# Attention and a token/channel mixer on one core: three stretches of small tiles in two steps, value products in seven pieces

## The chip, the cores and the metric

The kernel runs on one core of one Trainium2 chip. The metric is the device time of one execution in microseconds (us). Engines are named as in the profile: PE (TensorE, matrix products), DVE (VectorE), ACT (ScalarE), POOL (GpSimd) and SP (SyncE, which here only issues DMAs).

## The reference

A squared-ReLU attention over 8 batches, 12 heads, 448 positions and head size 64 feeds a mixer that works first over positions (tokens), then over channels.

```python
def _attn_ref(q, k, v):                      # (8, 12, 448, 64)
    scores = scale * np.matmul(q, k.transpose(0, 1, 3, 2))
    attn = np.maximum(scores, 0.0) ** 2 / S
    return np.matmul(attn, v).astype(np.float32)

def _moe_ref(x, w_tok1, w_tok2, w_ch1, w_ch2):   # x: (8, 448, 768), heads side by side
    xt = x.transpose(0, 2, 1)
    h = np.maximum(xt @ w_tok1, 0.0) @ w_tok2    # 448 -> 256 -> 448
    u = x + h.transpose(0, 2, 1)
    h2 = np.maximum(u @ w_ch1, 0.0) @ w_ch2      # 768 -> 1536 -> 768
    return (u + h2).astype(np.float32)
```

## The kernel before

**Steps.** The attention is cut into 24 steps of four heads; three steps make a batch. The operations of a step have short names that the text uses:

- `ld` loads q, k and v (POOL's queue, with the cast to bf16, two halves of 64 partitions each).
- `T` transposes q and k on PE for steps 0 to 7; its copies `cp` bring them from PSUM into `kqT`. From step 8 (`QDMA`) an interleaving copy on DVE (`i`) and a DMA transpose on SP (`x`) do this.
- `S` is a score tile, seven in a step (`KC`): four 64x64 products that run at once on the four quarters of PE and fill two PSUM banks. Each bank is emptied by a ReLU on ACT or DVE (`r`, lines 338 and 340), and DVE squares the pair (`q`, line 608) in one of 13 `sq` buffers.
- `V` is the value product: 28 products of 64x64 over the seven chunks, summed in two banks (line 629). In the kernel before it is one unit that needs all seven squares. Two evictions `xe` write `xT`.
- The token part: a transpose of `xT` (`X` on PE, from step 9 (`XDMA`) the DMA transpose `xd`), `t1` (line 745), `t2` (line 775), and the sum `u` on DVE; `ub` transposes u back by DMA on SP for the end.

**Channel part.** For each batch 12 products `C1` (line 837; six 128x128 matmuls of 448 columns each), and for each pair of batches 14 products `C2` (line 910; twelve matmuls a half). DVE adds u (line 926) and the result is stored (line 894). This is the large pool of work with 128x128 tiles that fills PE between the stretches of small tiles.

**The order.** The order of each engine's instructions is written by a planner (`Planner.run`, time steps of 0.01 us) when the kernel is built. Each operation has a duration, dependencies, and for DMAs a model of the rings that POOL and SP feed. PE's choice knows two shapes, "s" (64x64 tiles: T, S, V) and "m" (128x128). In shape "s" it goes on with values and scores that are ready and find banks; in shape "m" it takes large units until `since`, the time with large work, passes a bound that falls with the channel work in stock (between `FGAP` 0.5 and `GAP` 6 us), and then enters a stretch. The chip executes each engine's queue in the order so fixed, with semaphores where one engine needs another.

**Start and end.** In step 0 the first half of q comes by SP in fp32 (`load_first`, cast on DVE and ACT), the rest by POOL; the transposes of q and k of a half share a bank. The last output tile is stored in three pieces, each in two halves of partitions.

Of the kernel before, what the change touches and what calls it, by code (L numbers as in the profile page):

```python
# [18 lines left out]
QLATE, XLATE = 4.0, 6.0  # L19
FRONT, LOOKP, LOOKV = 40.0, 0.0, 0.0  # L20
VCUT = {}
RANKS = {}
CP_DVE = ()
# [3 lines left out]
HOLD = 1  # L27
STOCK, SLOPE, FGAP = 10.0, 0.4, 0.5
# [6 lines left out]
class Op:  # L35
    def __init__(self, name, eng, emit, deps=(), **kw):
        self.name, self.eng, self.emit = name, eng, emit
        self.deps = [d for d in deps if d is not None]
        self.on = None
        self.start = self.seen = None  # L40
        self.banks = 0
        self.bank = []
        self.frees = None
        self.rank = 0
        self.shape = None
        self.work = None
        self.durs = None
        self.late = None
        self.drain = self.adds = 0.0
        self.slack = 0.3  # L50
        self.__dict__.update(kw)
# [5 lines left out]
class Planner:  # L57
# [28 lines left out]
    def run(self, stream, gap, enter, tol, lanes=8):  # L86
# [27 lines left out]
        idle, filling = 0.0, None  # L114
        while left:
            self.moved(t, step)
            for e in ("POOL", "SP"):
# [12 lines left out]
                if o.work is not None:  # L130
                    issued[e] += 1
                    self.rings[e].append([t + o.dur + (1.13 if e == "POOL" else 0.135), o.work, o])
# [6 lines left out]
            for e in ("ACT", "DVE"):  # L139
# [3 lines left out]
                for o in self.open["FLEX"]:  # L143
# [4 lines left out]
                    key = (o.rank + (0 if e == o.eng else 100), o.at, o.n)  # L148
# [21 lines left out]
            if free["PE"] <= t:  # L170
# [19 lines left out]
                if shape == "s":  # L190
# [8 lines left out]
                else:  # L199
                    work, k = 0.0, -1  # L200
                    if va is not None and fits(va):
                        work += va.dur
# [37 lines left out]
                else:  # L240
# [5 lines left out]
                    if o is sc:  # L246
                        queue.pop(0)
                    if o is va:
                        values.pop(0)
# [19 lines left out]
def kernel(  # L269
# [84 lines left out]
    def load(s, t, halves=(0, 1)):  # L354
        src = {"k": k, "q": q, "v": v}[t]
        b, i = divmod(s, GS)
        for half in halves:
# [8 lines left out]
            o = add(Op(f"ld{t}{s}.{half}", "POOL", emit, dur=0.585, work=0.645, late=0.2 if s < 2 else None))  # L366
# [25 lines left out]
    def load_wc1(i, parts):  # L392
# [8 lines left out]
        o = add(Op(f"wc1.{i}", "POOL", emit, dur=0.9, work=12.0 / parts))  # L401
# [3 lines left out]
    def load_wc2(i, parts):  # L405
# [8 lines left out]
        o = add(Op(f"wc2.{i}", "POOL", emit, dur=0.9, work=10.65 / parts))  # L414
# [12 lines left out]
    def load_first():  # L427
        def emit(o):
            nc.sync.dma_start(out=q_first[:64], in_=q[0, :2].rearrange("e (p c) d -> p e (c d)", c=KC))

        ld = add(Op("ldf", "SP", emit, dur=0.5, work=0.9, late=0.1))
        for e in range(2):

            def emit(o, e=e):
                copy(o, raws["q"][0][:64, e], q_first[:64, e])

            o = Op(f"cast.{e}", ("DVE", "ACT")[e], emit, [ld], durs={"ACT": 0.58, "DVE": 0.4}, rank=-1)
            loads.setdefault((0, "q"), []).append(add(o))
# [3 lines left out]
    load(0, "q", (1,))  # L442
# [27 lines left out]
    def transpose(s, halves):  # L470
        def emit(o):
            o.ps = {}
            for i, half in enumerate(halves):
                o.ps[half] = bank(o, i, "kqT_ps").bitcast(BF16)
            for j, t in enumerate("kq"):
                r = raws[t][s % NR]
                for c in range(KC):
                    for half in halves:
                        rows = slice(64 * half, 64 * (half + 1))
                        for e in range(2):  # L480
                            nc.tensor.matmul(
                                o.ps[half][64 * e : 64 * (e + 1), j * S + c * KP : j * S + (c + 1) * KP],
                                lhsT=r[rows, e, c * D : (c + 1) * D],
                                rhs=ident[rows, rows],
                                is_transpose=True,
                                start=True,
                                stop=True,
                                skip_group_check=True,
                            )

        n = len(halves)
        if n == 1:
            deps = [loads[s, "k"][halves[0]]] + [o for o in loads[s, "q"] if (o.name == "ldq0.1") == halves[0]]
        else:
            deps = loads[s, "k"] + loads[s, "q"]
        dur = 0.63 if n == 1 else 0.465
        u = add(Op(f"T{s}.{halves[0]}", "PE", emit, deps, shape="s", banks=n, dur=dur))
        if n == 1:
            half = halves[0]
            got = []  # L500
            for j in range(2):
                got.append(
                    add(
                        Op(
                            f"cp{s}.{half}.{j}",
                            ("DVE", "ACT")[j],
                            lambda o, cols=slice(j * S, (j + 1) * S): copy(
                                o, kqT[half][s % NQ][:, cols], u.ps[half][:, cols]
                            ),
                            [u],  # L510
                            durs={"ACT": 0.45, "DVE": 0.35},
                            slack=0.3,
                            rank=1,
                            frees=lambda o: u.bank if all(x.start is not None for x in got) else [],
                        )
                    )
                )
            qkT_cp.setdefault(s, []).extend(got)
        else:
            for half in halves:  # L520
                qkT_cp.setdefault(s, []).append(
                    add(
                        Op(
                            f"cp{s}.{half}",
                            "DVE" if s in CP_DVE else ("ACT", "DVE")[half],
                            lambda o, half=half: copy(o, kqT[half][s % NQ], u.ps[half][:, : 2 * S]),
                            [u] + [sc[s - NQ, c] for c in range(KC) if s >= NQ],
                            durs={"ACT": 0.797, "DVE": 0.532},
                            slack=0.3,
                            rank=RANKS.get(("cp", s), 2.0),  # L530
                            frees=freed(u, half),
                        )
                    )
                )
# [5 lines left out]
    def crossing(s):  # L540
        for j, t in enumerate("kq"):

            def emit(o, j=j, t=t):
# [4 lines left out]
                Op(f"i{t}{s}", "DVE", emit, loads[s, t] + [cross.get((s - 1, t))], durs={"DVE": 0.534}, slack=9.0, rank=2)  # L548
            )

            def emit(o, j=j):
# [6 lines left out]
                Op(f"x{t}{s}", "SP", emit, [i] + [sc[s - NQ, c] for c in range(KC) if s >= NQ], dur=1.23, work=1.37, late=QLATE)  # L558
            )
            cross[s, t] = o  # L560
            qkT_cp.setdefault(s, []).append(o)

    def score(s, c):
        def emit(o):
            o.ps = [bank(o, e, "sc_ps") for e in range(2)]
            for half in range(2):
                for e in range(2):
# [16 lines left out]
        u = add(Op(f"S{s}.{c}", "PE", emit, qkT_cp[s], shape="s", banks=2, dur=0.189))  # L584
# [3 lines left out]
        old = vals.get((n - NSQ) // KC) if n >= NSQ else None  # L588
# [8 lines left out]
                    slack=0.2,  # L597
                    rank=RANKS.get(("r", s), 2.05),
# [3 lines left out]
            for e in range(2)  # L602
# [9 lines left out]
                rank=RANKS.get(("q", s), 2.1),  # L612
# [4 lines left out]
    def value(s):  # L617
# [20 lines left out]
        cut = VCUT.get(s, 0)  # L638
# [391 lines left out]
```

## Time and profile before

| what | value |
|---|---|
| median of the runs shown | 366.01 us (363.14, 366.01, 366.85) |
| the profiled execution: its own time | 364.49 us |
| its span, first to last instruction | 362.7 us, mean granted clock 0.995 |
| PE busy | 354.8 us, 98% |
| DVE, ACT, POOL busy | 231.6, 201.6, 91.6 us |
| channel products, L837 and L910 | 115.5 and 114.0 us of PE |
| score tiles, L575, and value products, L629 | 49.5 and 36.2 us of PE |
| ReLU evictions of scores: ACT, DVE | 258 and 78 |

A busy time counts overlapping instructions of an engine once, from the first's start to the last's end. In a timeline the rows merge neighbouring instructions of one kind: start, duration, engine, line, operation, output and inputs, shape, count. Where a row ends with a bracket, it gives the idle time of that engine before it and what ended it. A row of the waits gives the total, the number of times and the longest.

### The profile page before, as it was taken

The numbers are of one execution on the slowest core, as the hardware profiler recorded it, in microseconds if no ns is written. First come the engines' busy times: TensorE is split into PE (matmuls) and PEld (weight loads), VectorE is DVE, ScalarE is ACT, GpSimd is POOL, SyncE is SP. The second block draws the span as 40 slices with busy tenths as digits, with TensorE's granted clock in tenths as the row PEclk, the third lists the DMA queues.
The fourth block names the chain that finished last, engine by engine and source line by source line (L and its number), as shares of the span: only waits on it lengthen the run. The fifth ranks groups of instructions, "written<-read, shape, count | busy, mean of one in ns | idle before, by whom it ended". The sixth has DMA issues, their size and how long they took to land.

```text
span 362.7 us, 8725 instructions
## 1 busy us (share of the span) xinstructions
PE 354.8 (98%) x3475; PEld 197.0 (54%) x3475; DVE 231.6 (64%) x431; ACT 201.6 (56%) x419; POOL 91.6 (25%) x157
## 2 busy tenths in 40 slices
PE   7999999999999999999999999999999999999995
PEld 3555555655555554455555555555545555565563
DVE  2999587776899767999665585865656652030032
ACT  3999785546788257884567244762567413503300
POOL 8964414623243031543023030310000000000000
PEclk9899999999999999999999999999999999999999
DMA  7999999999999999999998979975422345031053
GB/s 113 186 197 201 198 193 161 176 169 198 133 142 178 219 145 158 188 131 214 165 196 127 198 147 219 122 109 106 108 54 52 75 103 115 1 74 44 0 122 96
DMA packets 98057, 50.18 MB, mean 138 GB/s; under 512 B 71968, under 2 KB 94560, under 8 KB 98016
## 3 DMA queue, kind: packets, MB, share of 16 engines
q1 hardware_dynamic: 73280, 27.87, 44.6%
q0 software_dynamic: 24496, 21.59, 42.6%
q8 instruction: 27, 0.44, 0.5%
q10 hardware_dynamic: 240, 0.16, 0.2%
q14 instruction: 14, 0.11, 0.1%
HBM read 43.38 MB, written 11.01 MB: 150 GB/s over the span
## 4 chain that ended last, share of the span: by engine, by line
PE 75%; DMA 16%; POOL 4%; DVE 1%; issue 1%; ACT 1%; POOLq 0%; ACTq 0%
PE m_ps L910 27%; PE m_ps L837 26%; DMA wc<-in_moe_w_ch_dram 9%; PE sc_ps L575 7%; PE acc_ps L629 6%; PE t_ps L745 5%; DMA q_raw<-in_q_dram 4%; PE h_ps L775 4%; DMA v_raw<-in_v_dram 3%; POOL k_raw L361 1%; POOL v_raw L361 1%; POOL q_raw L361 1%; DVE sq L340 0%; PE x_ps L715 0%; POOL wt L376 0%
## 5 line engine op out<-in xcount | busy, mean ns | idle before, releaser
L338 ACT ACTIVATE sq<-sc_ps 128x448 bf16<-128x448 f32 x258 | 122.5, 567 | 41.9 <-PE sc_ps L575 41.9
L837 PE MATMUL m_ps<-uT_sb,wc 128*128 128x448 bf16 x576 | 115.5, 353 | 0.2 <-DVE uT_sb L789 0.2
L910 PE MATMUL m_ps<-wc,r_sb 128*128 128x384 bf16 (+2 forms) x684 | 114.0, 323 | 0.1
L608 DVE TENSOR_TENSOR sq<-sq 128x896 bf16<-128x896 bf16 x168 | 98.8, 616 | 2.2 <-ACT sq L338 1.3
L910 PEld LDWEIGHTS <-r_sb 128*128 128x128 bf16 x684 | 65.8, 98 | 44.0 <-issue 2.0
L338 ACT ACTIVATE r_sb<-m_ps 128x448 bf16<-128x448 f32 x96 | 52.5, 550 | 58.2 <-PE m_ps L837 58.0
L837 PEld LDWEIGHTS <-wc 128*128 128x128 bf16 x576 | 55.2, 98 | 51.2 <-issue 3.3
L926 DVE TENSOR_TENSOR out_sb<-m_ps,u_sb 128x384 f32<-128x384 f32 (+2 forms) x57 | 31.2, 548 | 63.1 <-PE m_ps L910 63.1
L340 DVE TENSOR_SCALAR sq<-sc_ps 128x448 bf16<-128x448 f32 x78 | 46.6, 616 | 33.3 <-PE sc_ps L575 33.2
L361 POOL DMA_DIRECT2D v_raw<-in_v_dram x48 | 28.7, 606 | 125.3 <-PE sc_ps L575 116.9
L575 PE MATMUL sc_ps<-kqT 64*64 64x448 bf16 x672 | 49.5, 363 | 0.9 <-DVE sq L340 0.3
L789 DVE TENSOR_TENSOR uT_sb<-h_ps,xT 128x448 bf16<-128x448 f32 x48 | 28.1, 615 | 16.5 <-PE h_ps L775 16.4
L629 PE MATMUL acc_ps<-sq,v_raw 64*64 64x448 bf16 x672 | 36.2, 350 | 0.1
L361 POOL DMA_DIRECT2D k_raw<-in_k_dram x48 | 29.2, 622 | 15.3 <-DMA wc<-in_moe_w_ch_dram 12.6
L575 PEld LDWEIGHTS <-kqT 64*64 64x64 bf16 x672 | 17.4, 106 | 23.1 <-issue 17.1
L361 POOL DMA_DIRECT2D q_raw<-in_q_dram x47 | 28.9, 636 | 3.4 <-issue 1.7
L338 ACT ACTIVATE r_sb<-t_ps 128x512 bf16<-128x512 f32 (+1 forms) x27 | 15.5, 572 | 23.7 <-PE t_ps L745 23.7
L629 PEld LDWEIGHTS <-v_raw 64*64 64x64 bf16 x672 | 19.6, 107 | 12.8 <-issue 1.6
L745 PE MATMUL t_ps<-x_sb,wt 128*128 128x256 bf16 (+1 forms) x216 | 25.2, 261 | 0.6 <-ACT x_sb L344 0.3
L775 PE MATMUL h_ps<-wt,r_sb 128*128 128x448 bf16 x96 | 23.2, 354 | 0.0
L745 PEld LDWEIGHTS <-wt 128*128 128x128 bf16 x216 | 18.5, 98 | 8.1 <-issue 4.3
L660 ACT ACTIVATE xT<-acc_ps 128x448 bf16<-128x448 f32 x24 | 13.5, 562 | 9.6 <-PE acc_ps L629 9.2
(34 smaller groups left out, 107.8 us busy)
## 6 DMA issues: line engine op xcount, KB each, us to landing
out_dram<-out_sb SPq DMA_DIRECT2D x54, 192.0 KB, 2.9
k_raw<-in_k_dram POOLq DMA_DIRECT2D x48, 112.0 KB, 5.8
v_raw<-in_v_dram POOLq DMA_DIRECT2D x48, 112.0 KB, 5.1
q_raw<-in_q_dram POOLq DMA_DIRECT2D x47, 112.0 KB, 6.6
wc<-in_moe_w_ch_dram POOLq DMA_DIRECT2D x2, 1152.0 KB, 15.4
wc<-in_moe_w_ch_dram POOLq DMA_DIRECT2D x3, 768.0 KB, 14.4
u_sb<-uT_sb SPq DMA_TRANSPOSE x48, 5.1
kqT<-side SPq DMA_TRANSPOSE x32, 5.0
```

What stands on the lines that cost most here:

```text
L338: nc.scalar.activation(out, ps, AF.Relu)
L340: nc.vector.tensor_scalar(out=out, in0=ps, scalar1=0.0, scalar2=None, op0=ALU.max)
L361: nc.gpsimd.dma_start(out=raws[t][s % NR][64 * half : 64 * (half + 1)], in_=src[b, h0 : h0 + 2].rearrange("e (p c) d -> p e (c d)", c=KC),)
L575: nc.tensor.matmul(o.ps[e][64 * half : 64 * (half + 1), :S], lhsT=lhsT, rhs=rhs, start=True, stop=True, skip_group_check=True,)
L608: lambda o: nc.vector.tensor_tensor(out=buf, in0=buf, in1=buf, op=ALU.mult),
L629: nc.tensor.matmul(o.ps[half][64 * e : 64 * (e + 1), :S], lhsT=r[rows, e, c * D : (c + 1) * D], rhs=sq[rows, e, :], start=(c == 0), stop=( ...
L745: nc.tensor.matmul(o.ps[:, j, :], lhsT=wt1[:, c, j * 128 : (j + 1) * 128], rhs=x_sb[:, p0:p1, c, :], start=(c == 0), stop=(c == 3),)
L775: nc.tensor.matmul(o.ps[:, :S], lhsT=r1[:, j, a * 128 : (a + 1) * 128], rhs=wt2[:, j, :], start=(j == 0), stop=(j == JC - 1),)
L789: nc.vector.tensor_tensor(out=uTs[bb % 2][:, 2 * i + a, off : off + S].rearrange("n (c p) -> n c p", c=KC), in0=t2.ps[:, :S].rearrange("n ...
L837: nc.tensor.matmul(ps[:, :S], lhsT=wc1[:, g, e * 128 : (e + 1) * 128], rhs=uT[:, g, off : off + S], start=(g == 0), stop=(g == CC - 1),)
L910: nc.tensor.matmul(o.ps[:, :size], lhsT=r2[:, e, t * 128 : (t + 1) * 128], rhs=wc2[:, e, cols], start=(e == 0), stop=(e == EC - 1),)
L926: nc.vector.tensor_tensor(out=out_sb[:, cols].rearrange("n (g d) -> n g d", d=128), in0=u.ps[:, :size].rearrange("n (g d) -> n g d", d=128 ...
```

## The change

**In the planner's choice for PE, from step 12 (`ONE`) on.** `HEADS` names where a stretch may begin: in an even step before score tiles 0 and 5, in an odd step before tile 1. So stretches hold the score tiles (s.0 to s.4), then (s.5, s.6, s+1.0), then (s+1.1 to s+1.6), three for two steps. The value product of step s-1 belongs to the first, none to the second, that of step s to the third. The value product is cut into seven pieces of four products, one for each chunk, each of which waits for its own square; pieces and score tiles may alternate. Inside a stretch the planner prefers a score tile if banks are left, then a value piece, and goes over to large units after 0.3 us (`WAIT1`) without work, or when the next score tile is the head of another stretch. A stretch is entered when five banks are free (`NEED1`; three if the value's banks are taken) and all value pieces are ready within 0.8 us (`VSOON`), after 0.5 to 12 us of large work (`FGAP`, `GAP1`). Score evictions from step 12 on may go to ACT or DVE on equal terms (`away` 0, `RSL` 0). The release of an `sq` buffer follows the one value piece that reads it.

**In step 0.** Both halves of q come by SP and are cast on DVE and ACT (four casts); POOL's third load goes away. The transposes become four units in the order k and q of half 0, k and q of half 1, each with a bank of its own and one copy: ACT for k, DVE for q.

**In the transfer model.** New latencies (`PRE`, `POST`), a division of the DMA engines between the two rings (`SHARE`, `SHARE_W`) where it was even, and new times of work for several transfers. These change the order that the planner writes, not an instruction.

**At the end.** Of the second piece of the last tile one half is stored by SP where ACT stored both. Unused tables (`VCUT`, `RANKS`, `CP_DVE`) are gone.

```diff
-QLATE, XLATE = 4.0, 6.0
+QLATE, XLATE, ULATE = 4.0, 6.0, 0.5
+SHARE, SHARE_W = 0.35, 0.11
+PRE, POST = {"POOL": 1.5, "SP": 0.22}, {"POOL": 1.15, "SP": 1.07}
+RSL = 0.0
+HEADS = (((0, -1), (5, -2)), ((1, -1),))
+ONE, GAP1, WAIT1, NEED1, VSOON, IRANK = 12, 12.0, 0.3, 5, 0.8, 2.0
...
     def moved(self, t, step):
         heads = [q for q in self.rings.values() if q and q[0][0] <= t]
+        share = SHARE_W if heads and heads[0][0][2].name[:2] == "wc" else SHARE
         for q in heads:
-            q[0][1] -= step / len(heads)
+            q[0][1] -= step * (1.0 if len(heads) == 1 else share if q[0][2].eng == "SP" else 1.0 - share)
...
-                o.seen = t + (0.92 if o.eng == "POOL" else 1.15)
+                o.seen = t + POST[o.eng]
...
-                if shape == "s":
+                late = sc is not None and sc.name[0] == "S" and sc.step >= ONE
+                ends = late and sc.head and pick is not None
+                if late and va is not None and va.first is None and va.step > (vstep if shape == "s" and sc.head else sc.vstep):
+                    va = None
+                if shape == "s" and late:
+                    if not ends and fits(sc, va.banks if va is not None and va.ready(t + VSOON) else 0):
+                        o = sc
+                    elif va is not None and fits(va):
+                        o = va
+                    elif idle >= WAIT1 or sc.head and (va is None or not va.ready(t + VSOON)):
+                        o = pick
+                elif late and pick is not None and sc.head:
+                    soon = sc.ready(t) and n_free >= NEED1 - (2 if va is not None and va.first is not None else 0)
+                    if va is not None:
+                        soon = soon and all(v.ready(t + VSOON) for v in values if v.step == va.step)
+                    wait = min(max((self.stock - STOCK) * SLOPE, FGAP), GAP1)
+                    o = sc if soon and since >= wait else pick
+                elif shape == "s":
...
     def load_first():
-        def emit(o):
-            nc.sync.dma_start(out=q_first[:64], in_=q[0, :2].rearrange("e (p c) d -> p e (c d)", c=KC))
+        for half in range(2):
+            rows = slice(64 * half, 64 * (half + 1))
+
+            def emit(o, half=half, rows=rows):
+                nc.sync.dma_start(
+                    out=q_first[rows], in_=q[0, 2 * half : 2 * half + 2].rearrange("e (p c) d -> p e (c d)", c=KC)
+                )
...
     load(0, "k")
-    load(0, "q", (1,))
...
+    def transpose_first(half, j):
+        t = "kq"[j]
         def emit(o):
+            o.ps = bank(o, 0, "kqT_ps").bitcast(BF16)[:, :S]
+            for step in transposed(o.ps, 0, t, half):
+                step()
+        ...
+        u = add(Op(f"T0.{half}{t}", "PE", emit, deps, shape="s", banks=1, dur=0.32))
+        ...
+                    ("ACT", "DVE")[j],
+                    lambda o: copy(o, kqT[half][0][:, j * S : (j + 1) * S], u.ps),
...
+    def head(s, c):
+        starts = HEADS[(s - ONE) % len(HEADS)]
+        group = max([x for x in starts if x[0] <= c], default=HEADS[(s - 1 - ONE) % len(HEADS)][-1])
+        return dict(head=any(x[0] == c for x in starts), vstep=s + group[1] - (c < starts[0][0]))
...
-        old = vals.get((n - NSQ) // KC) if n >= NSQ else None
+        old = vals[n - NSQ] if n >= NSQ else None
...
-                    slack=0.2,
-                    rank=RANKS.get(("r", s), 2.05),
+                    slack=0.2 if s < ONE else RSL,
+                    away=100 if s < ONE else 0,
+                    rank=2.05,
...
-        cut = VCUT.get(s, 0)
-        parts = [list(range(cut)), list(range(cut, KC))] if cut else [list(range(KC))]
+        parts = [[c] for c in range(KC)] if s >= ONE else [list(range(KC))]
+        first = None
         for cs in parts:
...
-                loads[s, "v"] + [sq_ops[s, c] for c in cs] + [vals.get(s)],
+                loads[s, "v"] + [sq_ops[s, c] for c in cs],
                 shape="s",
                 banks=0 if cs[0] else 2,
                 dur=len(cs) * 0.189,
+                first=first,
+                step=s,
...
-                store(f"{n}.{i}", cols, [c2e[bb, t, i]], (("SP", "SP"), ("ACT", "ACT"), ("SP", "ACT"))[i])
+                store(f"{n}.{i}", cols, [c2e[bb, t, i]], (("SP", "SP"), ("SP", "ACT"), ("SP", "ACT"))[i])
...
-    stream = [transpose(0, [0]), transpose(0, [1])]
+    stream = [transpose_first(half, j) for half in range(2) for j in range(2)]
```

More of the change, by code (lines that the diff above doesn't have):

```diff
@@ L50, in __init__ @@
         self.slack = 0.3
+        self.away = 100
         self.__dict__.update(kw)
@@ new lines, in transposed @@
+    def transposed(out, s, t, half):
+        rows = slice(64 * half, 64 * (half + 1))
+        for c in range(KC):
+            for e in range(2):
+                yield lambda c=c, e=e: nc.tensor.matmul(
+                    out[64 * e : 64 * (e + 1), c * KP : (c + 1) * KP],
+                    lhsT=raws[t][s % NR][rows, e, c * D : (c + 1) * D],
+                    rhs=ident[rows, rows],
+                    is_transpose=True,
+                    start=True,
+                    stop=True,
+                    skip_group_check=True,
+                )
```

153 lines of the change are left out of this document (63 added, 90 removed).

## The prediction

> **What bounds the kernel now.** I read the page's first two parts, then the windows of the dense stretch, the list of waits there, and last the timeline of PE around single stretches, at the start and at the end. The page:
>
> ```profile
> PE 354.8 (98%) x3475; PEld 197.0 (54%) x3475; DVE 231.6 (64%) x431; ACT 201.6 (56%) x419; POOL 91.6 (25%) x157
> PE   7999999999999999999999999999999999999995
> DMA  7999999999999999999998979975422345031053
> ```
>
> PE is the bound from the second slice to the last. A busy PE isn't PE at its best, so the question is what its time holds besides products. The windows (PE, PEld, DVE, ACT, POOL busy with counts, then clock, DMA share, GB/s) and the waits between 137 us, where step 12 begins, and 303 us, where the last value product ends:
>
> ```profile
> 137.00:180.00 43.00, 42.94 (x441) 23.31 (x444) 38.16 (x71) 30.52 (x66) 14.26 (x24) 1.00 1.24 177
> 180.00:220.00 40.00, 40.00 (x328) 22.19 (x316) 26.59 (x50) 20.35 (x43) 10.67 (x18) 1.00 0.99 162
> ...
> ACT sq L338 <- PE sc_ps L575: 30.8, 13, 5.9
> ...
> PEld L575 <- issue: 8.8, 26, 0.4
> ```
>
> No PE row stands in that list: nothing that PE works on comes late there. DVE and ACT wait for PE, with room to spare after 180 us but little before (DVE 38.16 of 43). The 26 in the last line is the number of times that PE goes from large tiles into a stretch of small ones. What such a stretch costs is in the timeline (start, duration; starts are what count, since durations overlap):
>
> ```profile
> 185.21 1.30 PE L837 MATMUL m_ps<-uT_sb,wc 128*128 128x448 bf16 x6
> 186.43 0.76 PE L575 MATMUL sc_ps<-kqT 64*64 64x448 bf16 x12
> 187.13 0.93 PE L775 MATMUL h_ps<-wt,r_sb 128*128 128x448 bf16 x4
> 187.90 5.84 PE L837 MATMUL m_ps<-uT_sb,wc 128*128 128x448 bf16 x30
> 193.66 0.57 PE L575 MATMUL sc_ps<-kqT 64*64 64x448 bf16 x8
> 194.07 1.49 PE L629 MATMUL acc_ps<-sq,v_raw 64*64 64x448 bf16 x28
> 195.39 0.55 PE L575 MATMUL sc_ps<-kqT 64*64 64x448 bf16 x8
> 195.87 2.44 PE L837 MATMUL m_ps<-uT_sb,wc 128*128 128x448 bf16 x12
> ```
>
> Going in: six products from 185.21 to 186.43 take 1.22; undisturbed, 60 of them take from 303.28 to 314.63, 0.189 each, so six are 1.135 and the entry costs 0.085. Coming out: twelve small products take from 186.43 to 187.13, 0.70; in the value product 28 take 1.32 (194.07 to 195.39), 0.047 each, so twelve are 0.565, and the exit costs 0.135. **A stretch costs 0.22 us**, however long it is: the mixed one (193.66 to 195.87, 44 products) has 2.21 - 2.07 = 0.14 at its exit too.
>
> The Trainium skill, TensorEngine Tiling (Array Packing), Key Properties, says that changing the tiling mode drains TensorE; the rows agree, with 0.22 for the pair of changes.
>
> **1. Fewer stretches.** Between 137 and 303 us there are 26. The new heads give three for every two of the 12 steps, 18, plus the tail end of step 11 and the lone last value product: 20. Six fewer at 0.22 is **-1.3 us**. The sum of products stays the same. If the new order leaves stretches before their end (its rule lets it go over to large tiles after 0.3 us without work), the count may not fall at all: bounds -1.3 and 0.
>
> **2. What waits inside the longer stretches.** Now the most scores at a time are two, a value product of 1.32 us, and two more. In the new form a stretch holds five or six score tiles with the seven value pieces between them, or three alone. A score tile takes two PSUM banks that come free only when ACT or DVE has read them. At the start of the profile four ACT evictions take 1.85, (1.85 - 0.55) / 3 = 0.43 each, and two DVE ones 1.16, 0.54 each; together a half tile every 0.24. Of eight banks two hold the value sums, so six hold three score tiles, and the sixth tile waits for the third's two halves. First eviction some 0.44 after the first tile begins (0.19 of products and about 0.25 until ACT starts, as between 186.43 and the like), six half tiles 1.44, release 0.18: 2.06, and about 0.2 more for the large product that was still to be evicted, 2.26. PE arrives there after five scores and seven value pieces, 12 x 0.189 = 2.27. So it just fits, with nothing to spare; the stretch of five tiles has half a microsecond to spare. One DVE operation of 0.55 in the way makes it a wait of 0.27. Each value piece is also a wait of PE on one square of DVE, 84 where there were 12; behind each on PE's queue stand the next scores and all large products. The squares were made a stretch earlier, so they should be done. I take 0.035 for each of the 12 long stretches, **+0.4 us**; bounds 0 and 12 x 0.3 = 3.6, the wait that the order itself tolerates.
>
> The same page of the Trainium skill, PSUM Bottleneck, warns that tiling speeds up TensorE but not the emptying of PSUM, and wants both engines on it. By that rule alone the longer stretches would be paid for at the evictions' pace; that is the second rival below.
>
> **3. Changing between scores and values.** About eight changes in each long stretch. Two scores before a value take 0.41 (193.66 to 194.07) for 0.377 of products: at most 0.03 a change. But the mixed stretch costs as much over its products as the plain one, within 0.01. I take **+0.2**; bounds 0 and 12 x 8 x 0.03 = 2.9.
>
> **4. The first transposes.** The rows:
>
> ```profile
> 5.39 0.54 ACT L344 ACTIVATE kqT<-kqT_ps 128x448 bf16<-128x448 bf16 x1 [0.60 <-PE kqT_ps L481]
> 5.96 0.39 DVE L346 COPY kqT<-kqT_ps 128x448 bf16<-128x448 bf16 x1 [1.37 <-ACT kqT L344]
> ...
> 6.70 0.41 PE L481 MATMUL kqT_ps<-ident,q_raw 64*64 64x64 bf16 x14 [0.17 <-DMA q_raw<-in_q_dram]
> ...
> 7.15 0.55 ACT L344 ACTIVATE kqT<-kqT_ps 128x448 bf16<-128x448 bf16 x1 [1.22 <-PE kqT_ps L481]
> ...
> 7.73 0.39 DVE L346 COPY kqT<-kqT_ps 128x448 bf16<-128x448 bf16 x1 [1.37 <-ACT kqT L344]
> ```
>
> Both copies of a half read one bank, and DVE's starts when ACT's ends. The second ends at 8.12 and the scores go on. Four transposes with a bank each let the copies run together, and the last q half no longer comes third on POOL's queue but second on SP's, with two more casts (0.39 on DVE, 0.58 on ACT, as those at 4.21) that lie in the wait for the second k half, which PE meets at 6.13. From there: k 0.32, q 0.32, copy of q about 0.1 later and 0.39 long: 7.26 in place of 8.12. POOL has one issue fewer ahead of everything else, 0.60 (two take 1.21). Against that, q's second half competes with the first k loads, the DMA engines are full from about 3 us on, and if the copies wait for each other by their target and not by the bank, 0.55 stays. From 31 us PE is dense, and what the start gains reaches the end only as far as loads and weights arrive earlier too. I take **-0.6**; bounds -1.0 and +0.5.
>
> The Trainium skill, Trainium Kernel Development and Optimization, Key Constraints, says that DMAs from SP, ACT and POOL share the same 16 engines and that issuing from several saves only issue time; by it the gain would stop at the 0.60 of one POOL issue, which my value doesn't pass.
>
> **5. The last stores.**
>
> ```profile
> 358.34 1.91 ACTq L894 DMA_DIRECT2D out_dram<-out_sb  x3
> 358.55 0.29 DVE L926 TENSOR_TENSOR out_sb<-m_ps,u_sb 128x128 f32<-128x128 f32 x1 [0.24 <-PE m_ps L910]
> ```
>
> The last result is there at 358.84, but ACT is issuing until 360.25, 0.64 a store. One of the three moves to SP, which has time between its issues. **-0.5**; bounds -0.64 and 0.
>
> **6. The transfer model.** New figures for DMA times change no instruction, only the order that the planner writes out, also in steps 0 to 11. PE idles little for late transfers now, so there is little to mend: **0**. An order with seven stretches more or fewer before 137 us would be worth 7 x 0.22: bounds -1.5 and +1.5.
>
> **Sum.** -1.3 + 0.4 + 0.2 - 0.6 - 0.5 + 0 = **-1.8 us**. The profiled execution took 364.49 (span 362.7), so 362.7. The median of the runs shown is 366.01, 1.5 above it; the saving carried over gives **364.2**.
>
> **Rivals.** *More is gained.* All of the start reaches the end (-1.0), the waits stay at nothing, and the new order also drops stretches before step 12 (-1.5): -1.3 - 1.0 - 0.64 - 1.5 = -4.4, **361.6**. For it: the 19 changes of tile size that the timeline shows between 100 and 148 us. Against: nothing in the diff aims at those steps. Chance 0.30.
>
> *Evictions take over.* In the long stretches DVE's squares stand in its queue ahead of evictions, and ACT alone empties the banks, 0.87 a tile. Now ACT does 258 of the 336 evictions. The fifth tile then waits until 0.44 + 2 x 0.87 + 0.18 = 2.36 in place of 1.9 and the sixth until 3.23 in place of 2.27; over six stretches of each kind 0.46 x 6 + 0.96 x 6 = 8.5. With the 2.4 gained elsewhere (parts 1, 4 and 5) that is +6.1: **372.1**. It decides from a wait of 2.4 / 12 = 0.2 a long stretch on; from 0.5 the kernel is measurably slower. For it: DVE is busy 38.16 of 43 us in the first steps concerned. Against: from step 12 evictions may go to DVE on equal terms, and after 180 us it is busy for only two thirds. Chance 0.14.
>
> *Nothing comes of it.* Stretches are left early and entered again, so the count stays near 26, or the larger bound on large work between stretches (12 us for 6) lets the last value product slip. It ends at 302.5 now, channel products of the last batch start at 327.15, and the way between them through transpose and token products needs some 15, so it may slip by 9 us without a loss. About the tail alone remains: **365.5**. Chance 0.13.
>
> **How the numbers follow.** The forecast has 0.43 and its own range is 362.3 to 366.5. A measurement of this kernel tells about 1% (3.7 us) from no change: the runs before spread over that much. Faster by more than that needs 362.35: the first rival and a little of the forecast, 0.32. Slower needs 369.7: the second rival, 0.13. Within 1%: 0.55. The range for 8 in 10 takes in the first rival and part of the second: 360.6 to 368.6.
>
> **What would show it.** Right: the line of PEld waits at L575 counts near 20 between step 12 and the last value product; value products come in pieces of four between scores; no PE row of waits on ACT or DVE there; the first scores run on by 7.5 us; the last ACT issue ends near 359.6. Wrong: PE waits for L338, L340 or L608 in the long stretches, more than 0.2 each; as many stretches as before; a gap in PE after the last value product.

## The result, and the profile after

The changed kernel takes **362.19 us** (median of 22 runs), the kernel before 364.98 beside it (22 runs): a ratio of **0.9925, interval 0.990 to 0.995**, some 2.7 us. The forecast was 364.2 for a kernel before of 366.01, a saving of 1.8. Of the profiles below, three are of executions more than 1.5% longer than the fastest of their kernel (the first with the stretches undone, the new order alone, the long stretches from step 4 on), and what they show is told of those executions only.

The profiled executions show where it is: spans of 362.7 and 359.8. The page after:

```profile
PE 352.0 (98%) x3473; PEld 199.9 (56%) x3473; DVE 245.6 (68%) x460; ACT 189.7 (53%) x392; POOL 91.1 (25%) x156
PE   7999999999999999999999999999999999999995
```

PE is as full as before, DVE does more and ACT less. Since a busy share can't tell a product from a change of tile size, I use a second measure, the **excess**: time on PE less every matmul of the computation at its pace in undisturbed rows (0.189 us for 448 columns, 0.1625 for 384, 0.109 for 256, 0.0555 for 128, 0.047 for a 64x64 product of 448, 0.008 for a 64x64 transpose). Filling and warm-up products count as excess. Both kernels do the same products, so differences of excess are differences of time. It is read from starts, so it also holds waits that the list of waits doesn't show. By stage, with the number of stretches of small tiles in brackets:

| stage | before | after | difference |
|---|---|---|---|
| start to the first score of step 5 | 19.04 | 19.03 | -0.01 |
| step 5 to step 12 | 4.67 (17) | 3.75 (16) | -0.92 |
| step 12 to PE's last product | 6.44 (26) | 4.91 (19) | -1.53 |
| from there to the end of the span | 4.19 | 3.72 | -0.47 |

They add up to -2.93. From the waits of the same 137 to 303 us as before (total, times, longest); again no PE row is among them:

```profile
ACT sq L360 <- PE sc_ps L608: 22.7, 8, 8.3
DVE sq L362 <- PE sc_ps L608: 10.0, 7, 2.3
PEld L608 <- issue: 6.0, 17, 0.4
```

The entries that this line catches fall from 26 to 17 (the timeline has 19 stretches). One of the new long ones:

```profile
184.72 0.57 PE L608 MATMUL sc_ps<-kqT 64*64 64x448 bf16 x8
185.13 0.74 PE L663 MATMUL acc_ps<-sq,v_raw 64*64 64x448 bf16 x12
185.69 0.36 PE L608 MATMUL sc_ps<-kqT 64*64 64x448 bf16 x4
185.88 0.36 PE L663 MATMUL acc_ps<-sq,v_raw 64*64 64x448 bf16 x4
186.07 0.36 PE L608 MATMUL sc_ps<-kqT 64*64 64x448 bf16 x4
186.26 0.36 PE L663 MATMUL acc_ps<-sq,v_raw 64*64 64x448 bf16 x4
186.45 0.36 PE L608 MATMUL sc_ps<-kqT 64*64 64x448 bf16 x4
186.64 0.55 PE L663 MATMUL acc_ps<-sq,v_raw 64*64 64x448 bf16 x8
187.12 3.20 PE L871 MATMUL m_ps<-uT_sb,wc 128*128 128x448 bf16 x16
```

Five scores and seven value pieces, 48 products, from 184.72 to 187.12: 2.40, of which products at 0.047 are 2.26. The 0.14 left is what the exit of a short stretch cost before. Each score comes 0.38 after the last without a wait, and the alternation costs nothing that can be seen.

The start, where the prediction had expected 0.6:

```profile
6.09 0.57 ACT L366 ACTIVATE q_raw<-side 64x448 bf16<-64x448 f32 x1 [1.09 <-DMA side<-in_q_dram]
6.09 0.39 DVE L368 CAST q_raw<-side 64x448 bf16<-64x448 f32 x1 [1.28 <-DMA side<-in_q_dram]
6.42 0.41 PE L500 MATMUL kqT_ps<-ident,k_raw 64*64 64x64 bf16 x14 [0.97 <-DMA k_raw<-in_k_dram]
6.76 0.23 PE L1022 MATMUL fill_ps<-warm 128*128 128x128 bf16 x1
7.05 0.41 PE L500 MATMUL kqT_ps<-ident,q_raw 64*64 64x64 bf16 x14
7.49 0.39 DVE L368 COPY kqT<-kqT_ps 128x448 bf16<-128x448 bf16 x1 [0.59 <-PE kqT_ps L500]
```

The second q half lands at 6.09 and is cast until 6.66. The second k half lands later than before, at 6.42 in place of 6.13. Behind its transposes the order has a filling product of 128x128 at 6.76 (the planner writes these where it expects PE to wait), and only then, at 7.05, the transposes of q; before, these ran at 6.70. They come 0.62 or 0.63 behind those of k in the eight profiles at full pace that have this filling product, and 0.24 behind in the one whose order has none there, that with the old transfer figures:

```profile
6.33 0.41 PE L500 MATMUL kqT_ps<-ident,k_raw 64*64 64x64 bf16 x14 [0.72 <-DMA k_raw<-in_k_dram]
6.57 0.39 PE L500 MATMUL kqT_ps<-ident,q_raw 64*64 64x64 bf16 x14
```

The copies no longer wait for each other, which wins the delay back, and no more: the last copy ends at 7.88 (8.12 before), but PE is through with the first scores at 9.80 (9.81 before).

### The profile page after: what moved, and what is told of

It reads as the page before. It is cut to its first block, busy times and chain, and to the rows that moved or that the text cites. A ratio compares the mean times of both kernels' runs of the same rounds, so it can differ in the third digit from the quotient of the medians.

```text
span 359.8 us, 8764 instructions
## 1 busy us (share of the span) xinstructions
PE 352.0 (98%) x3473; PEld 199.9 (56%) x3473; DVE 245.6 (68%) x460; ACT 189.7 (53%) x392; POOL 91.1 (25%) x156
## 4 chain that ended last, share of the span: by engine, by line
PE 88%; DMA 3%; POOL 2%; DVE 2%; ACT 2%; issue 2%; DVEq 0%; ACTq 0%; POOLq 0%
PE m_ps L944 31%; PE m_ps L871 29%; PE sc_ps L608 8%; PE acc_ps L663 7%; PE t_ps L779 6%; PE h_ps L809 5%; DMA q_raw<-in_q_dram 3%; ACT sq L360 2%; POOL k_raw L383 1%; DVE sq L642 1%; DVE sq L362 1%; PE x_ps L749 1%; PE kqT_ps L500 1%; POOL q_raw L383 0%; POOL v_raw L383 0%
## 5 line engine op out<-in xcount | busy, mean ns | idle before, releaser
L360 ACT ACTIVATE sq<-sc_ps 128x448 bf16<-128x448 f32 x230 | 110.1, 576 | 39.3 <-PE sc_ps L608 39.2
L642 DVE TENSOR_TENSOR sq<-sq 128x896 bf16<-128x896 bf16 x168 | 97.7, 618 | 2.2 <-ACT sq L360 1.6
L362 DVE TENSOR_SCALAR sq<-sc_ps 128x448 bf16<-128x448 f32 x106 | 61.4, 617 | 20.5 <-PE sc_ps L608 20.5
L608 PE MATMUL sc_ps<-kqT 64*64 64x448 bf16 x672 | 51.9, 361 | 0.5
L663 PE MATMUL acc_ps<-sq,v_raw 64*64 64x448 bf16 x672 | 41.1, 350 | 0.1
L608 PEld LDWEIGHTS <-kqT 64*64 64x64 bf16 x672 | 19.5, 106 | 20.4 <-issue 13.4
L809 PE MATMUL h_ps<-wt,r_sb 128*128 128x448 bf16 x96 | 22.7, 354 | 0.1
```

The lines of the kernel that those rows point to most:

```text
L360: nc.scalar.activation(out, ps, AF.Relu)
L362: nc.vector.tensor_scalar(out=out, in0=ps, scalar1=0.0, scalar2=None, op0=ALU.max)
L608: nc.tensor.matmul(o.ps[e][64 * half : 64 * (half + 1), :S], lhsT=lhsT, rhs=rhs, start=True, stop=True, skip_group_check=True,)
L642: lambda o: nc.vector.tensor_tensor(out=buf, in0=buf, in1=buf, op=ALU.mult),
L663: nc.tensor.matmul(o.ps[half][64 * e : 64 * (e + 1), :S], lhsT=r[rows, e, c * D : (c + 1) * D], rhs=sq[rows, e, :], start=(c == 0), stop=( ...
L809: nc.tensor.matmul(o.ps[:, :S], lhsT=r1[:, j, a * 128 : (a + 1) * 128], rhs=wt2[:, j, :], start=(j == 0), stop=(j == JC - 1),)
```

## The experiments

Each kernel is the changed one with one edit, unless told otherwise. The ratio is to the kernel before in the same job. Stages come from one profile each.

### The stretches undone, twice

```diff
-ONE, GAP1, WAIT1, NEED1, VSOON, IRANK = 12, 12.0, 0.3, 5, 0.8, 2.0
+ONE, GAP1, WAIT1, NEED1, VSOON, IRANK = 99, 12.0, 0.3, 5, 0.8, 2.0
```

> The changed kernel with the three-in-two stretches, the value pieces and the equal terms for evictions undone (ONE from 12 to 99); start, stores and transfer model as changed. Theory one (the time from step 12 on is saved by going into small tiles less often, at about 0.22 us each): 26 stretches from step 12 on in place of 19, so 7 x 0.22 = 1.5 us more than the changed kernel, profiled span near 361.3 us, and no PE waits that explain it. Rival (the order written with the new transfer model saves it, the stretches pay for themselves at best): within 0.5 us of the changed kernel, span 359.5 to 360.3.

> The same kernel as the first with the stretches undone (ONE 99), for a profile in which the clock isn't cut in the middle. What is compared is the excess from the first score of step 12 to PE's last product: that time less every matmul at its pace in undisturbed rows. It was 6.44 us with 26 stretches before and 4.91 with 19 in the changed kernel. Theory one (0.22 for each stretch): 26 stretches and 4.91 + 7 x 0.22 = 6.4. Rival (the excess falls by the order that the transfer model gives, or by the evictions' equal terms): 5.0 to 5.5.

Ratios 0.9986 (0.994 to 1.003) and 1.0038 (0.999 to 1.009): the gain is gone. The first profile has PE waiting 2.7 us on a DMA transpose from about 156 us on and half the clock in two places, so its 10.56 from step 12 on can't be compared. The second has 26 stretches and an excess of 7.47, in which one wait stands out:

```profile
168.33 0.57 PE L608 MATMUL sc_ps<-kqT 64*64 64x448 bf16 x8 [0.84 <-DMA kqT<-side]
```

That stretch costs 1.0 more than others; without it 6.4 is left, what theory one expected, and the rival's 5.0 to 5.5 is out. Span and ratio lie further off than 1.5 us. The profiled execution also waits between steps 5 and 12 (7.67 in place of 3.75), where the order is that of the changed kernel, so this isn't the edit's doing; more on it below. That the others of this kernel wait there too isn't shown.

### Four stretches for two steps

```diff
-HEADS = (((0, -1), (5, -2)), ((1, -1),))
+HEADS = (((0, -1), (4, -2)),)
```

> The changed kernel with four stretches for two steps (heads before score tiles 0 and 4 of each step, the value product in the first), pieces and the rest as changed. Theory one: 24 or 25 stretches from step 12 on, excess there 4.91 + 5.5 x 0.22 = 6.1 (5.9 to 6.3), so 1.2 us more than the changed kernel. Rival (shorter stretches win back what the long ones wait): 4.9 to 5.4.

Excess from step 12 on 6.23 with 25 stretches; the stages ahead of it as in the changed kernel (3.76 from step 5 on). 6.23 - 4.91 = 1.32 for six stretches: **0.22 each**. Ratio 0.998 (0.993 to 1.003). This is the cleanest of the runs: pieces, evictions and start are kept, and only the number of stretches and their length differ. It is the stage in the profile that shows it; the interval of the ratio still touches that of the changed kernel.

### One stretch a step

```diff
-HEADS = (((0, -1), (5, -2)), ((1, -1),))
+HEADS = (((0, -1),),)
```

> The changed kernel with one stretch a step (seven scores with the seven value pieces of the step before). Theory one taken on its own: 13 stretches, excess from step 12 on 4.91 - 6 x 0.22 = 3.6. Theory two (evictions bind from here on: a half tile every 0.24 us, six banks, so the seventh score waits for the fourth's banks until 0.44 + 8 x 0.24 + 0.18 + 0.2 = 2.74 where PE arrives at 2.46, and DVE's squares stand between): waits of 0.3 or more a stretch, or stretches left early; excess 5.5 to 8, so no gain over the changed kernel.

Excess 6.95 and 19 stretches, ratio 1.0015 (0.997 to 1.007). Theory two: the order leaves a stretch when banks run out, and what it doesn't leave waits.

```profile
194.45 0.57 PE L608 MATMUL sc_ps<-kqT 64*64 64x448 bf16 x8
194.86 0.74 PE L663 MATMUL acc_ps<-sq,v_raw 64*64 64x448 bf16 x12
195.42 1.30 PE L608 MATMUL sc_ps<-kqT 64*64 64x448 bf16 x12
196.51 0.40 PE L663 MATMUL acc_ps<-sq,v_raw 64*64 64x448 bf16 x4
196.85 3.42 PE L944 MATMUL m_ps<-wc,r_sb 128*128 128x384 bf16 x20
```

Here 36 products take 2.40, 0.70 more than their 1.70: scores that follow scores go at the evictions' pace. The six stretches that do hold seven scores and seven pieces take 3.01 for 56 products, 0.24 more than products and an exit. The list of PE's waits is empty in this run too, from 137 to 303 us, so an empty list is no sign that nothing waits; the starts of the rows tell it. Six scores between seven pieces is what two evicting engines keep up with.

### Value products in one unit

```diff
-        parts = [[c] for c in range(KC)] if s >= ONE else [list(range(KC))]
+        parts = [list(range(KC))]
```

> The changed kernel with each value product of step 12 on in one unit of 28 matmuls again, heads and the rest as changed. Theory one (the pieces are what makes a long stretch possible: they give ACT and DVE time between scores): with the unit in one block the scores after it find banks late, stretches wait or are left and entered again; 24 or more stretches from step 12 on and an excess there of 6.0 to 6.5. Rival (the heads alone do it; pieces don't matter): 19 or 20 stretches, excess 4.9 to 5.3.

26 stretches, excess 7.94, ratio 1.002 (0.997 to 1.007). Worse than theory one had it, because the mixed stretches also wait:

```profile
222.59 0.57 PE L608 MATMUL sc_ps<-kqT 64*64 64x448 bf16 x8
223.00 1.49 PE L663 MATMUL acc_ps<-sq,v_raw 64*64 64x448 bf16 x28
224.32 0.74 PE L608 MATMUL sc_ps<-kqT 64*64 64x448 bf16 x12
225.12 1.03 PE L779 MATMUL t_ps<-x_sb,wt 128*128 128x256 bf16 x8
```

The same 48 products as in the changed kernel's stretch above take 2.53 in place of 2.40. By the sum over banks, scores on either side of a block of 1.32 us have banks for two or three tiles, then none; spread out, each score finds a pair free. Eleven more stretches of this form than in the changed kernel, at 0.13 each, and seven stretches more at 0.22 are 3.0, about what is lost.

### Evictions to ACT first

```diff
-                    slack=0.2 if s < ONE else RSL,
-                    away=100 if s < ONE else 0,
+                    slack=0.2,
+                    away=100,
```

> The changed kernel with score evictions from step 12 on given to ACT first again, as in the steps before. Theory two (the evictions are what a long stretch stands on; DVE must take its share on equal terms): the sixth score tile waits or stretches are left early, 21 or more stretches and an excess from step 12 on of 5.8 to 7. Rival (ACT has the room, busy 25 of 43 us after 137 us): 19 or 20 stretches, excess 4.9 to 5.2.

Excess 6.66 with 22 stretches, ratio 0.996 (0.991 to 1.002): theory two. Three stretches more are 0.66; the rest is waiting in the stretches of six:

```profile
178.81 0.36 PE L663 MATMUL acc_ps<-sq,v_raw 64*64 64x448 bf16 x4
179.00 0.53 PE L608 MATMUL sc_ps<-kqT 64*64 64x448 bf16 x4
179.58 0.73 PE L871 MATMUL m_ps<-uT_sb,wc 128*128 128x448 bf16 x3
```

The sixth score takes 0.58 to the next product where 0.19 of products and an exit of about 0.13 would do. DVE does 38 of the 168 evictions from step 12 on here, 70 in the changed kernel. So ACT's idle time over the whole stage is no help within 2.5 us; DVE's share is.

### The old figures of the transfer model

```diff
-QLATE, XLATE, ULATE = 4.0, 6.0, 0.5
-SHARE, SHARE_W = 0.35, 0.11
-PRE, POST = {"POOL": 1.5, "SP": 0.22}, {"POOL": 1.15, "SP": 1.07}
+QLATE, XLATE, ULATE = 4.0, 6.0, 1.0
+SHARE, SHARE_W = 0.5, 0.5
+PRE, POST = {"POOL": 1.13, "SP": 0.135}, {"POOL": 0.92, "SP": 1.15}
...
```

> The changed kernel with the old figures of the transfer model (latencies, even division of the engines, works, late 1.0 for the u transposes). No instruction differs, only the order. Theory one (the 0.9 us gained between steps 5 and 12 come from the order that the new figures give, a stall of 0.64 us at 82 us and a stretch less): about 0.9 us more than the changed kernel, lost before step 12, by a stall or stretches there; span near 360.7. Rival (that part comes by chance from any change in the start): the time before step 12 as in the changed kernel, span within 0.4 us of it.

Ratio 0.9946 (0.991 to 0.999), which overlaps the changed kernel's. From step 12 on 4.98 with 20 stretches, as in the changed kernel. Before step 12 the excess adds up to 17.80 + 6.36 = 24.2, against 22.8 there and 23.7 in the kernel before: the loss is where theory one put it, 1.4 rather than 0.9, though this start ran at full clock and won 1.2 us. Of PE's listed waits between steps 5 and 12, 1.5 us are for DVE and 0.4 for the q load of step 6. The longest:

```profile
94.39 0.62 DVE L573 COPY side<-k_raw 128x896 bf16<-128x896 bf16 x1 [3.85 <-DMA kqT<-side]
94.93 0.61 DVE L362 TENSOR_SCALAR sq<-sc_ps 128x448 bf16<-128x448 f32 x1
95.59 1.29 PE L871 MATMUL m_ps<-uT_sb,wc 128*128 128x448 bf16 x6 [0.96 <-DVE sq L362]
```

DVE's interleaving copy waits for a DMA transpose that still reads its buffer, and an eviction stands behind the copy. The kernel before has the like with a load:

```profile
83.16 0.62 DVE L545 COPY side<-k_raw 128x896 bf16<-128x896 bf16 x1 [2.93 <-DMA q_raw<-in_q_dram]
83.56 0.54 PE L575 MATMUL sc_ps<-kqT 64*64 64x448 bf16 x5
83.70 1.14 DVE L340 TENSOR_SCALAR sq<-sc_ps 128x448 bf16<-128x448 f32 x2
...
84.37 0.38 PE L575 MATMUL sc_ps<-kqT 64*64 64x448 bf16 x3 [0.27 <-DVE sq L340]
```

DVE's next instruction is an interleaving copy whose load isn't there; it waits 2.93 us, the evictions queue behind it, and PE stops for a bank. That stretch costs 0.64 more than its like. The changed kernel's DVE has no wait for a DMA between 60 and 110 us. That the planner puts the copy further back because it takes loads to land later is likely, but no run changes that figure alone.

### The new order from step 12 on, alone

The start, the transfer model and the stores as in the kernel before; only the stretches, pieces and equal terms are new.

> The new order from step 12 on alone: start, transfer model and stores as in the kernel before. Theory one (the parts add up): excess from the first score of step 12 to PE's last product 4.91 + 0.22 for each stretch over 19, so near 5.3 with 21; the way from PE's last product to the end 4.2 as before; between steps 5 and 12 as in the kernel before, 4.7, if the loads come as they did there. So 1.1 us less than the kernel before. Rival (the new order needs the new transfer figures, without them its stretches wait): excess from step 12 on 6.0 or more, no gain.

Ratio 0.9965 (0.993 to 1.000), 1.3 us. The start took 22.3 in this execution, at half clock from 12.4 to 22.7 us. Step 5 to 12 has 4.79, with the stall of DVE's copy again (the stretch at 85.1 costs 0.66 over its products where its like costs 0.14), and PE's last product to the end 4.20. From step 12 on the excess is 7.20 with 20 stretches, of which 1.94 is one stretch where DVE and PE wait; the other 5.26 is what theory one expected. As it stands 7.20 is in the rival's range, whose "no gain" the ratio doesn't bear out; one profile with one such wait can't say whether the old figures invite it.

### The old start

> The changed kernel with the transposes and q loads of step 0 as before (second q half by POOL, one bank for both copies). Theory one (the new start gives nothing by itself, since step 5 begins at 49.1 us in both kernels): step 5 begins within 0.2 us of 49.1; whatever differs behind that comes from another order, by 0.22 for each stretch more or fewer. Rival (the start's gain of up to 0.6 is there, and hidden by something in the new order): step 5 begins 0.4 us later or more.

Excess up to step 5 18.87, where the changed kernel has 19.03 and the kernel before 19.04: no difference that can be seen in the start, as theory one had it. Its sign failed, for step 5 begins at 51.7, but because another unit stands ahead of it in this order; the excess is what compares. All three starts had one stage at half clock. Behind it the order differs, with 4.04 and 5.11 in place of 3.75 and 4.91. Ratio 0.996 (0.993 to 1.000).

### The old stores

```diff
-                store(f"{n}.{i}", cols, [c2e[bb, t, i]], (("SP", "SP"), ("SP", "ACT"), ("SP", "ACT"))[i])
+                store(f"{n}.{i}", cols, [c2e[bb, t, i]], (("SP", "SP"), ("ACT", "ACT"), ("SP", "ACT"))[i])
```

> The changed kernel with both halves of the last tile's second piece stored by ACT again. Theory one: PE's last product ends when it does in the changed kernel (356.1), and the way from there to the end of the span is 4.2 us in place of 3.7: span 0.45 us longer, near 360.3. Rival (the last stores land at the same time, since the transfers share their engines): span as in the changed kernel within 0.1.

4.14 from PE's last product to the end, 3.72 in the changed kernel: 0.42, theory one. After (first) and with the old stores:

```profile
355.88 1.21 ACTq L928 DMA_DIRECT2D out_dram<-out_sb  x2
```

```profile
360.23 1.91 ACTq L928 DMA_DIRECT2D out_dram<-out_sb  x3
```

The span is 364.5, though steps 5 to 12 and all from 12 on are as in the changed kernel (3.75 and 4.91): the start took 23.38 in place of 19.03, for a reason that the last section tells. Ratio 0.995 (0.991 to 0.999).

### Long stretches from step 4 on

```diff
-ONE, GAP1, WAIT1, NEED1, VSOON, IRANK = 12, 12.0, 0.3, 5, 0.8, 2.0
+ONE, GAP1, WAIT1, NEED1, VSOON, IRANK = 4, 12.0, 0.3, 5, 0.8, 2.0
```

> The changed kernel with the new stretches from step 4 on in place of 12, as a version that may be better. Theory one: the order has 56 stretches in all in place of 58, so about 0.4 us less, if nothing waits: excess from step 5 to PE's last product 8.2 in place of 8.66. Rival (before step 12 loads bound PE, so fewer stretches there only move the wait to the loads): no gain, waits of the step 6 to 9 transposes on their loads in place of it.

No gain: ratio 0.9995 (0.995 to 1.004), eight of twelve executions at 366.4 or more. Neither theory named what stands out in the profile:

```profile
193.49 0.62 DVE L573 COPY side<-q_raw 128x896 bf16<-128x896 bf16 x1 [5.38 <-DMA kqT<-side]
194.03 1.14 DVE L362 TENSOR_SCALAR sq<-sc_ps 128x448 bf16<-128x448 f32 x2
194.69 0.58 PE L608 MATMUL sc_ps<-kqT 64*64 64x448 bf16 x3 [4.50 <-DVE sq L362]
```

It is the copy on DVE again, here behind a DMA transpose that still reads its buffer, and PE waits 4.5 us for the eviction queued behind it. That the other executions lose their time in this way isn't shown. Between steps 5 and 12 there are three stretches fewer (13), and 4.76 all the same.

### Filling products in the first waits

```diff
+            if half:
+                ps = bank(o, 0, "fill_ps")
+                for _ in range((14, 3)[j]):
+                    nc.tensor.matmul(ps[:, :128], lhsT=warm[:, :128], rhs=warm[:, :128], start=True, stop=True)
             o.ps = bank(o, 0, "kqT_ps").bitcast(BF16)[:, :S]
```

> The changed kernel with 14 more filling products ahead of the transposes of the second k half and 3 ahead of those of the second q half, where PE was idle for 0.97 us; nothing else. Theory of the clock (the 3.41 us at half clock from 7.6 us on follow the idle time, and cost 1.1 us up to step 5): no half-clock stage in the profile, step 5 begins near 48.0 us at an excess of 17.8 in place of 19.0. Theory of the loads (step 6 to 8 wait for loads behind the weights, so an earlier PE only waits longer there): the excess from step 5 to 12 rises by 0.8 or more from 3.75, and the whole gains 0.3 or less. Rival: the half-clock stage comes all the same.

No half-clock stage after the first scores, but in this execution the clock rose only at about 6.5 us, the first transposes ran at half speed, and the start came to 19.28, not 17.8 (which counts the 17 added products). Between 5 and 12 the excess is 5.06: PE waits 0.98 for the q load of step 6. Ratio **0.989 (0.985 to 0.993)**, the best of all, over six runs from 361.3 to 363.1; the interval overlaps that of the changed kernel, so it isn't shown to be better.

## Why the prediction was right

- **The bound and the price of a stretch** held: PE, and 0.22 us, which the run with four stretches measures again at 0.22. There were seven fewer and not six; 7 x 0.22 is all of the 1.53 saved from step 12 on. The forecast for parts 1 to 3 together was 0.7.
- **Waits in the long stretches (+0.4)** came to about 0.35: nine of the twelve cost 0.14 over their products, as a short one does, and three cost 0.18, 0.27 and 0.32. But the kernel before had a wait of its own that the sum left out: twelve products took 0.95 (154.52 to 155.47) where others take 0.70. So the net is 0.1. **Alternation (+0.2)** cost nothing that can be seen. The sum over banks was right to its edge: six scores just fit with both engines evicting (0.24 us a half tile), they wait when ACT goes first, and seven don't fit.
- **The start (-0.6)** failed: it came to nothing. The working began with the second k half at 6.13 and put q's transposes 0.32 behind k's. The k half landed at 6.42, 0.29 later (6.14 to 6.83 in ten profiles with both q halves on SP, 6.13 or 6.14 in three with one; that the second q load holds it up is likely, not shown), and the filling product put q's transposes 0.63 behind. The two make up the 0.6, and the sign "the first scores run on by 7.5 us" failed: they began at 8.16. Of the profiles with one stage at half clock in the start, six with the new start have 18.7 to 19.2 up to step 5 and two with the old 18.9 and 19.0.
- **The last stores (-0.5)** gave 0.47, 0.42 when put back alone.
- **The transfer model (0)** was wrong in a way that helped in this profile: 0.92 between steps 5 and 12, of which 0.64 is the stall and 0.22 a stretch. "PE idles little for late transfers" was read from PE's waits; the stall there stood as a wait for DVE, whose own wait was for a load. For the kernel at large the 0.92 isn't shown, as the next paragraphs tell.

The misses are -0.8 from step 12 on, -0.9 between steps 5 and 12, and +0.6 in the start. That they cancel in part is luck, and the sum of 1.8 still falls 1.1 short of the 2.9 in the profiles. The time of 364.2 lies 2.0 above 362.19; half of that is its base, three runs at 366.01 where 22 gave 364.98. The measured time is just below the forecast's own range (362.3 to 366.5) and inside the range for 8 in 10. As a time it is nearer to *More is gained* (361.6), as a saving nearer to the forecast (2.8 between the medians, against 1.8 and 4.4).

*Evictions take over* is a real mechanism, but it was priced too high: 0.46 for a stretch of five scores and 0.96 for one of six, where with ACT first four of six scores waited 0.30 each and those of five 0 to 0.13. In that run DVE still did 38 evictions, so ACT never was alone. The change brings its own remedy, the equal terms. *More is gained* looked for 1.5 before step 12 from fewer stretches; one stretch went away there.

The excess between 5 and 12 isn't the same in all executions of one order: 3.75 or 3.76 in four profiles of orders that agree up to step 12, 4.5 to 7.8 in five, while the order of the kernel before has 4.67 and 4.79 in two. Where it is more, PE waits for loads of step 6, which POOL issues behind the weights:

```profile
59.50 0.59 POOL L383 DMA_DIRECT2D k_raw<-in_k_dram  x1 [3.68 <-DMA wc<-in_moe_w_ch_dram]
...
60.99 0.22 PE L500 MATMUL kqT_ps<-ident,k_raw 64*64 64x64 bf16 x2 [0.53 <-DMA k_raw<-in_k_dram]
62.14 0.41 PE L500 MATMUL kqT_ps<-ident,k_raw 64*64 64x64 bf16 x26 [0.93 <-DMA k_raw<-in_k_dram]
```

This is the second run with the stretches undone; in the changed kernel's profile POOL issued that load at 57.43 and PE didn't wait. The two of the nine that reached step 5 soonest (17.8 and 17.9) wait longest, and then lose more to a stage at half clock. So what a faster start wins is likely taken back here; that the loads are the cause of the spread in general is argued, not tried.

## What to carry to other kernels

Price a change of tile mode from start-to-start times of neighbouring rows, count the changes, and the gain of merging stretches follows; how long a stretch may be follows from banks and the pace of both evicting engines. On an engine that executes in order, look at what waits ahead of an eviction: a copy placed before its load has landed stops another engine, and the list of waits then names the wrong one. When several terms are added, a sum that comes out is no proof of the terms; undo them one by one.

## What the runs showed of the hardware

I had not looked at the clock at the start. PE's granted clock falls to half there for a stage of 3.41 us in most profiles, for three such stages in a row (10.24) in one, and in others not at all. From 8 to 12 us it was (PE busy with counts, other engines, PEclk, DMA, GB/s) in the kernel before and with the old transfer figures:

```profile
8.00:12.00 4.00, 3.85 (x83) 2.01 (x81) 2.62 (x6) 2.71 (x6) 3.98 (x7) 0.57 1.18 177
```

```profile
8.00:12.00 4.00, 3.61 (x95) 2.13 (x84) 3.97 (x8) 4.00 (x9) 4.00 (x7) 1.00 1.18 165
```

One such stage costs some 1.2 us up to step 5 (excess 19.0 against 17.8; 0.8 to 1.5 over the profiles). In the run with the old stores the rows are at half pace until about 23.6 us (28 transposes take 0.59 there, 0.41 at full pace), though the clock column shows 1.00 in that time, and that start cost 4.35 more than the changed kernel's: over 1% of the kernel, more than the whole change. Executions of the kernel before lie between 363.1 and 368.5; how much of that is the clock isn't shown, since its stages are known for the profiled executions alone. The Trainium skill, TensorE: Matmul & The Clock Gate, Part 1, describes a free-running window of 3.4 us whose phase varies from run to run, which fits the 3.41 us and a start of the stage that lies between 7.3 and 8.3 us in eight profiles. Its estimate that the ramp stays under 1% of a typical kernel holds here for one such stage, and not for the execution with the old stores.

A stage came without 3.41 us of idle time: where PE was busy 2.25 and 2.24 of 4 us (60 to 64 us in the two runs with the stretches undone), the next 4 us had a mean clock of 0.58 and 0.67. Where it was busy 3.04 of 4 us (200 to 204 us in the run with the new order alone), the clock stayed at 1.00. But busy time alone doesn't tell: from 4 to 8 us it was 3.23 in the kernel before, and a half-clock stage followed, and 3.07 with the old transfer figures, where none did. So a wait of PE of some two microseconds can be paid for again at half pace.
